# One instruction per 128 columns for scale, table and maximum of a windowed softmax, with slope tables that stay and a written order drawn up anew

## The chip, the core and the metric

The kernel runs on one core of a Trainium2 chip. The metric is the device time of one execution in microseconds, as the median of several runs. Five engines work side by side, each on its own queue in its own order: TensorE (PE; its weight loads are shown apart as PEld), VectorE (DVE), ScalarE (ACT), GpSimd (POOL) and SyncE (SP), which only issues transfers here.

## The reference, cut to what matters

```python
def _attn_ref(q, k, v):                      # 4 x 8 heads, 576 positions, 64 wide
    scores = scale * q @ k^T                 # scale = 1 / sqrt(64) = 0.125
    rel = pos[:, None] - pos[None, :]
    slopes = 2.0 ** (-8.0 * (arange(H) + 1) / H)      # 2 ** -(head + 1) for 8 heads
    scores = where((rel >= 0) & (rel < 128), scores - slopes * abs(rel), -1e9)
    attn = exp(scores - max(scores))
    return (attn / (sum(attn) + 1e-9)) @ v

x = heads side by side                       # 2304 x 512
x = (sigmoid(x @ w_gate) * (x @ w_val)) @ w_out       # 12 slices of 128 columns
out = ((x @ w1) * (x @ w2)) @ w3 @ w_out2
```

## The kernel before

The 2304 rows are 18 tiles of 128, in five blocks of 2, 4, 4, 4 and 4 tiles (`TILES`). Attention runs in 20 steps n = 0 to 19: five blocks times four pairs of heads (n = 4 * block + pair). `stage_s(n)` computes the scores of a step in sub-steps of two tiles and two heads, so n = 0 to 3 have one sub-step and the other 16 steps two each: 36 sub-steps. Of a sub-step the scores s lie in PSUM as two key blocks per tile. VectorE (1) copies with a mask, so that one block of 128 columns per tile and head holds the 128 keys of the window (L797, letter m), (2) multiplies 512 columns by the scale and adds a table (L801, letter t), (3) takes the maximum over 128 columns for four rows at once (L808, letter x), and for pairs 1 to 3 scales that maximum (L812). ScalarE takes four exponentials of 128 columns with their sums (L816, letter e). VectorE forms the reciprocal of the sums (L820, L821, letter s), GpSimd and ScalarE multiply by it (L826, L828, letter n). `stage_p` (L836) transposes the result on TensorE, ScalarE copies it out and GpSimd cuts it into its own and the previous key block; `stage_pv` multiplies by v into pv, and the result is split into a high part xth and a low part xtl, the sum of which is the input x of the first layer.

The table (`table`, `fill_table`) is made per block: for a block's 2 or 4 tiles and the two heads of pair 0. The other pairs use the same table: their scores are multiplied by 4 ** pair on the way in, and the exponential divides again. It takes 18 instructions of 128x256, 2 on ScalarE for block 0 and 16 on GpSimd.

Weights come as 64-bit words. `rounded` turns 128 rows of 512 of them into 32 bit numbers: one step on ScalarE (L195, letter a) and six on VectorE (L197 to L202, letter r), called a conversion below; then high and low parts are written (`wsl`, on ScalarE and GpSimd, letter c), or the result goes back to memory for later (`early`, from SP, letter u). The raw words are fetched by SP (L173, letter w). A name such as a_(6, 0) is slice 6 of the first layer, weight 0 (gate), and a_('ahead', 'o2', 3) a weight that is only needed later.

The first layer runs by groups of weight slices: slice 0, slice 1, then (2, 3), (4, 5) and so on, each over the five blocks. `gv` makes two products (L412), ScalarE a tanh of the first, and VectorE combines it with the second into g (L434, letter g), which sets its PSUM bank free. `down1` multiplies by the third weight into dn (L452) and VectorE adds it up in acc (L460, L462, letter d). Slices 0 and 1 run as fillers among the attention steps on TensorE.

What sets the order: TensorE follows the order of the program during attention. For the other engines `TURNS` holds one string of letters per engine; `line_up` chains the instructions marked by `turn` in the order of the letters, and a scheduler places everything else. Before, `line_up` is called when the fillers are done, ahead of the loop over the groups from (2, 3) on. From there the scheduler decides.

## Time and profile before

| | us |
|---|---|
| runs, median of 3 (lowest, highest) | 891.55 (889.65, 892.42) |
| the profiled execution | 895.77 |
| its span | 894.1 |

The profile is of the one execution of 895.77 us, 4.2 us above the median; 1.7 us of it lie outside the span. It tells for each engine when an instruction ran and what ended the idle time before it. "PEclk" is the clock that TensorE was granted, as a share of its higher level.

### The profile page before, as it was taken

How to read it: one execution, taken by the hardware profiler on the slowest of the kernel's cores; microseconds unless marked ns; L12 is line 12 of the kernel's file. 1: busy time of each engine (PE TensorE's matmuls, PEld its weight loads, DVE VectorE, ACT ScalarE, POOL GpSimd, SP SyncE). 2: the span in 40 equal slices, each digit the busy share in tenths (PEclk: the TensorE clock that was granted, in tenths of full speed). 3: DMA queues.
4: the chain of work that ended last, by engine and by line, in shares of the span. 5: the costliest groups of instructions: out<-in, count | busy, mean ns of one | idle time of the engine just before them, and what ended most of it. 6: DMA issues, size and time to landing. Idle time of an engine off the chain costs nothing.

```text
span 894.1 us, 12465 instructions
## 1 busy us (share of the span) xinstructions
PE 868.7 (97%) x4432; PEld 714.3 (80%) x4432; DVE 661.8 (74%) x1156; ACT 351.4 (39%) x853; POOL 311.7 (35%) x352
## 2 busy tenths in 40 slices
PE   6789999999999999999999999999999999999998
PEld 4567777788878888888888888878788888888886
DVE  5989997599997994994898954595548887643434
ACT  6888877432323322322422433342333424222120
POOL 4776664533315313322511211114535542021121
PEclk9999999999999999999999999999999999999999
DMA  5535441323451430350145421048434355654322
GB/s 172 177 124 183 157 161 56 128 79 123 154 179 56 167 128 1 122 178 20 67 162 181 152 87 48 25 148 299 167 140 166 118 199 201 223 189 154 136 77 95
DMA packets 40046, 120.61 MB, mean 135 GB/s; under 512 B 4400, under 2 KB 6448, under 8 KB 37936
## 3 DMA queue, kind: packets, MB, share of 16 engines
q1 hardware_dynamic: 38688, 105.01, 34.7%
q10 hardware_dynamic: 1296, 14.81, 3.9%
q8 instruction: 35, 0.57, 0.3%
q14 instruction: 27, 0.22, 0.1%
HBM read 87.82 MB, written 31.98 MB: 134 GB/s over the span
## 4 chain that ended last, share of the span: by engine, by line
PE 75%; DVE 16%; DMA 4%; issue 3%; ACT 1%; POOL 1%; SPq 0%; ACTq 0%; DVEq 0%; POOLq 0%
PE gv L412 22%; PE o L642 11%; PE dn L452 11%; PE pb L523 9%; PE pd L523 5%; PE pv L861 4%; PE w3o L373 3%; PE s L788 3%; PE lone L616 3%; PE pc L523 2%; PE pt L836 2%; DVE acc L462 2%; DVE g L434 1%; DMA _('ahead', 'w3', 4)_4938<-in_w_dram 1%; DVE xf L107 1%
## 5 line engine op out<-in xcount | busy, mean ns | idle before, releaser
L412 PE MATMUL gv<-xth,wsl 128*128 128x512 f32 (+1 forms) x960 | 281.9, 371 | 3.4 <-DVE g L434 2.8
L412 PEld LDWEIGHTS gv<-xth,wsl 128*128 128x128 f32 x960 | 175.9, 190 | 38.5 <-DVE g L434 3.8
L412 PE MATMUL gv<-xtl,wsl 128*128 128x512 f32 (+1 forms) x480 | 177.5, 370 | 1.5 <-DVE xtl L107 1.5
L110 POOL TENSOR_TENSOR gt<-g,gt 128x512 fp32r<-128x512 f32 (+1 forms) x60 | 77.4, 1290 | 240.2 <-ACT gt L104 240.2
L452 PE MATMUL dn<-gt,wsl 128*128 128x512 f32 (+1 forms) x720 | 154.5, 368 | 0.0
L452 PEld LDWEIGHTS dn<-gt,wsl 128*128 128x128 f32 x720 | 125.8, 189 | 23.4 <-DVE su L820 0.3
L412 PEld LDWEIGHTS gv<-xtl,wsl 128*128 128x128 f32 x480 | 91.3, 190 | 16.1 <-DVE xtl L107 1.7
L523 PE MATMUL pb<-xf,forms 128*128 128x512 f32 x384 | 97.8, 391 | 0.0
L462 DVE TENSOR_TENSOR acc<-acc,dn 128x512 f32<-128x512 f32 (+1 forms) x120 | 73.1, 625 | 16.3 <-PE dn L452 16.1
L523 PEld LDWEIGHTS pb<-xf,forms 128*128 128x128 f32 x384 | 70.8, 188 | 14.9 <-ACT xb L104 0.5
L434 DVE SCALAR_TENSOR_TENSOR g<-g,gv 128x512 f32<-128x512 f32 (+1 forms) x60 | 37.4, 627 | 44.1 <-PE gv L412 44.0
L104 ACT ACTIVATE gt<-g 128x512 fp32r<-128x512 f32 (+1 forms) x60 | 35.1, 587 | 80.0 <-DVE g L434 79.9
L816 ACT ACTIVATE sm<-sm,mn 128x128 f32<-128x128 f32 x144 | 56.1, 392 | 14.3 <-DVE mn L812 11.0
L652 DVE TENSOR_TENSOR acc<-acc,o 128x512 f32<-128x512 f32 x54 | 36.8, 683 | 32.8 <-PE o L642 32.7
L110 POOL TENSOR_TENSOR tp<-x,tp 128x512 fp32r<-128x512 f32 x16 | 21.2, 1325 | 86.8 <-ACT tp L104 86.7
L523 PE MATMUL pd<-xf,forms 128*128 128x512 f32 x192 | 48.9, 390 | 0.8 <-DVE xb L566 0.8
L642 PE MATMUL o<-outw,tp 128*128 128x512 f32 x192 | 48.0, 390 | 0.3 <-POOL tp L110 0.3
L642 PE MATMUL o<-outw,tq 128*128 128x512 f32 x192 | 48.2, 389 | 0.0
L427 ACT ACTIVATE g<-gv 128x512 f32<-128x512 f32 (+1 forms) x60 | 32.5, 547 | 34.3 <-PE gv L412 29.7
L373 PE MATMUL w3o<-wo,w3s 128*128 128x512 f32 x192 | 44.4, 390 | 0.4 <-ACT w3s L104 0.4
L523 PEld LDWEIGHTS pd<-xf,forms 128*128 128x128 f32 x192 | 36.0, 188 | 8.7 <-DVE xb L566 1.3
L826 POOL TENSOR_SCALAR sm<-sm,su 128x128 f32<-128x128 f32 x72 | 29.3, 416 | 38.5 <-DVE su L821 27.3
(797 smaller groups left out, 1467.1 us busy)
## 6 DMA issues: line engine op xcount, KB each, us to landing
formd<-forms ACTq DMA_DIRECT2D x8, 1792.0 KB, 7.4
outw<-outd SPq DMA_DIRECT2D x16, 512.0 KB, 5.6
forms<-formd SPq DMA_DIRECT2D x8, 1024.0 KB, 5.1
ldk<-in_k_dram SPq DMA_DIRECT2D x16, 320.0 KB, 3.5
ldv<-in_v_dram SPq DMA_DIRECT2D x16, 320.0 KB, 3.8
out_dram<-acc SPq DMA_DIRECT2D x18, 256.0 KB, 2.0
ldq<-in_q_dram SPq DMA_DIRECT2D x16, 256.0 KB, 4.4
outd<-w3o SPq DMA_DIRECT2D x8, 512.0 KB, 2.9
```

The costliest lines, as they stand in the source:

```text
L104: return nc.scalar.activation(dst, src, AF.Copy)
L110: nc.gpsimd.tensor_tensor(dst, src, hi.bitcast(F32), ALU.subtract)
L373: nc.tensor.matmul(acc2, w3s[u][:, wp, i * P : (i + 1) * P], wo2[kk][:, xp], start=(kk == 0 and wp == 0 and xp == 0), stop=(kk == NC2 - 1 ...
L412: nc.tensor.matmul(ps, wsl[i][:, s, wp, kk * P : (kk + 1) * P], xs[blk][xp][:, kk], start=(kk == 0 and wp == 0 and xp == 0), stop=(kk == N ...
L434: nc.vector.scalar_tensor_tensor(pr, pr, 1.0, pss[i, 1], ALU.add, ALU.mult)
L452: nc.tensor.matmul(ps, wsl[i][:, 2, wp, m * P : (m + 1) * P], t[:, xp], start=n == 0, stop=n == 3 * len(grp) - 1,)
L462: nc.vector.tensor_tensor(a, a, ps, ALU.add)
L523: nc.tensor.matmul(ps, forms[i][:, a, wp, kk * P : (kk + 1) * P], xf[n, j][:, xp, kk], start=first and kk == 0 and (wp, xp) == PASSES[0], ...
L642: nc.tensor.matmul(ps, ts2[n, i][blk][:, xp, tt * P : (tt + 1) * P], outw[i][:, wp], start=k == 0, stop=k == 3 * len(grp) - 1,)
L652: nc.vector.tensor_tensor(a, a, ps, ALU.add)
L816: nc.scalar.activation(y, y, AF.Exp, bias=mn[:, j : j + 1], scale=1.0 / up, accum_out=su[:, j : j + 1])
L861: nc.tensor.matmul(ps[c, a:b], loads[n]["v"][:, j + 1, c], s["cp", h][:, m0 : m0 + b - a], start=j == -back, stop=j == nt - 1, skip_group_ ...
```

## The change

`tensor_reduce`, the scaling of the maximum and `scalar_tensor_tensor` go. In their place stand four `tensor_tensor_reduce` per sub-step, one for each 128 columns: each adds a table to the scores, multiplies by -0.125 and takes the minimum, which is the negated maximum. The built program shows each as two VectorE instructions, one of 128x128 and one of 128x1 that writes the minimum. The factor 4 ** pair is gone; instead each head has a table `slope` of its own, with one 128-column part for each of the four kinds of tile, made once. It takes 16 instructions of 128x256: 2 on ScalarE, 14 on GpSimd, nearly all at the very start. `base` has 4 parts instead of 7, so three copies on ScalarE go. `TURNS` is drawn up anew, and `line_up` comes two groups later, after group (4, 5), so that the written order now also covers groups (2, 3) and (4, 5).

```diff
-        "mxtsxxogsmsdtxsxddssdsosgdddoorrdrrdrdrrgddrrgdddrrdrgdddd"
+        "rggdddd"
+LINED = 3
...
-        base = spool.tile([P, 7, P], F32, name="base", bufs=1)
-        PAIRS = {"nf": 0, "fn": 1, "nn": 2, "nc": 3, "ca": 4, "an": 5}
+        base = spool.tile([P, 4, P], F32, name="base", bufs=1)
+        slopes = [cpool.tile([P, 4, P], F32, name=f"slope{head}") for head in range(2 * NPAIR)]
...
+        def table(pair, kinds):
+            for head in (2 * pair, 2 * pair + 1):
+                c = 8.0 * 2.0 ** -(head + 1)
+                to, by = slopes[head][:, kinds], base[:, kinds]
+                with turn("T"):
+                    if pair == 0 and kinds.start == 0:
+                        nc.scalar.activation(to, by, AF.Copy, scale=c)
+                    else:
+                        nc.gpsimd.tensor_scalar(to, by, c, 1.0, ALU.mult, ALU.mult)
...
                 with turn("t"):
-                    nc.vector.scalar_tensor_tensor(
-                        x[:, g].rearrange("p g u k -> p g (u k)"), ps[:, :, 1].rearrange("p g u k -> p g (u k)"),
-                        0.125 * up, tabs[blk][:, g].rearrange("p g u k -> p g (u k)"), ALU.mult, ALU.add,
-                    )
+                    for j in range(4):
+                        head, u = 2 * pair + j // 2, j % 2
+                        kind = "fnca".index(KINDS[t0 + 2 * tp + u])
+                        nc.vector.tensor_tensor_reduce(
+                            x[:, 2 * tp + j // 2, u], ps[:, j // 2, 1, u], slopes[head][:, kind],
+                            -0.125, 3.0e38, ALU.add, ALU.min, mn[:, j : j + 1],
+                        )
-                with turn("x"):
-                    nc.vector.tensor_reduce(
-                        mn, x[:, g].rearrange("p g u k -> p (g u) k"), axis=AX.X, op=ALU.max, negate=True
-                    )
-                    if pair:
-                        nc.vector.tensor_scalar(mn, mn, 1.0 / up, None, ALU.mult)
...
-                            y, y, AF.Exp, bias=mn[:, j : j + 1], scale=1.0 / up, accum_out=su[:, j : j + 1]
+                            y, y, AF.Exp, bias=mn[:, j : j + 1], scale=-1.0, accum_out=su[:, j : j + 1]
...
-        table(0)
+        for pair in range(NPAIR):
+            table(pair, slice(0, 2))
...
                         consts2()
-                if n % NPAIR == NPAIR - 2 and n // NPAIR + 1 < NBLK:
-                    table(n // NPAIR + 1)
+                    for pair in range(NPAIR):
+                        table(pair, slice(2, 4))
...
     while queue:
         convert_next()
-    line_up()
...
             convert(1 if blk == 0 else 3)
+        if gi == LINED:
+            line_up()
```

What the written order does is seen at three places. The first is VectorE at step n = 8, from its first masked copy on. Before (s_0_707 and s_1_712 are its two sub-steps, sm the softmax tile, mn the maxima, su the sums):

```order
L797 COPY_PREDICATED s_0_707<-mask,s_0_707 128x2x256
L820 TENSOR_SCALAR su_1_623<-su_1_623 128x4
L821 RECIPROCAL su_1_623<-su_1_623 128x4
L801 SCALAR_TENSOR_TENSOR sm_706<-s_0_707,tab_475 128x512
L797 COPY_PREDICATED s_1_712<-mask,s_1_712 128x2x256
L808 TENSOR_REDUCE mn_0_719<-sm_706 128x4
L197 TENSOR_SCALAR a_(1, 0)_655<-a_(1, 0)_655 128x512
L801 SCALAR_TENSOR_TENSOR sm_706<-s_1_712,tab_475 128x512
```

After, where the tiles are s_0_730, s_1_735, sm_729 and mn_0_741, and the second copy of each pair of heads' rows that read alike is left out:

```order
L789 COPY_PREDICATED s_0_730<-mask,s_0_730 128x2x256
L113 TENSOR_TENSOR xtl_611<-pv_716,xth_610 128x512
L798 ISA sm_729,mn_0_741<-s_0_730,slope_94 128x128
L798 ISA mn_0_741 128x1
...
L798 ISA sm_729,mn_0_741<-s_0_730,slope_95 128x128
...
L789 COPY_PREDICATED s_1_735<-mask,s_1_735 128x2x256
```

Two 512-column instructions per sub-step became four pairs. Ahead of this place stand 7 conversions now (the seventh but for its last step), those of slices 0 and 1 and of a_('ahead', 2, 0), where 3 stood before; the conversion of a_(1, 0), which begins here before, is long done.

The second place is VectorE in group (2, 3) of the first layer at the g of block 4 (its two slices). Before:

```order
L201 SCALAR_TENSOR_TENSOR s_(6, 1)_3277<-raw_(6, 1)_3150,s_(6, 1)_3277 128x512
L202 TENSOR_TENSOR a_(6, 1)_3276<-a_(6, 1)_3276,s_(6, 1)_3277 128x512
L200 TENSOR_SCALAR s_(7, 1)_3290<-a_(7, 1)_3289 128x512
L201 SCALAR_TENSOR_TENSOR s_(7, 1)_3290<-raw_(7, 1)_3164,s_(7, 1)_3290 128x512
L202 TENSOR_TENSOR a_(7, 1)_3289<-a_(7, 1)_3289,s_(7, 1)_3290 128x512
L434 SCALAR_TENSOR_TENSOR g_4_2850<-g_4_2850,gv_4_1_2854 128x512
L434 SCALAR_TENSOR_TENSOR g_4_2852<-g_4_2852,gv_4_1_2871 128x512
```

After (g_4_2893 and g_4_2895):

```order
L468 TENSOR_TENSOR acc_2_1698<-acc_2_1698,dn_2_2_2818 128x512
L440 SCALAR_TENSOR_TENSOR g_3_2764<-g_3_2764,gv_3_1_2768 128x512
L440 SCALAR_TENSOR_TENSOR g_3_2766<-g_3_2766,gv_3_1_2785 128x512
L440 SCALAR_TENSOR_TENSOR g_4_2893<-g_4_2893,gv_4_1_2897 128x512
L208 TENSOR_TENSOR a_('ahead', 'o2', 3)_2857<-a_('ahead', 'o2', 3)_2857,s_('ahead', 'o2', 3)_2858 128x512
L203 TENSOR_SCALAR a_('ahead', 'o2', 4)_2963<-a_('ahead', 'o2', 4)_2963 128x512
```

The g of block 4 moved ahead of the conversions of slices 6 and 7 and of three of the 'ahead' weights; these now come in group (4, 5).

The third place is the head of SP's queue, which issues the first transfers. Before:

```order
L751 DMA ldk_95<-in_k_dram 128x128
L752 DMA ldk_95<-in_k_dram 128x256
L173 DMA raw_(0, 0)_111<-in_w_gate_dram 128x1024
L764 DMA boot<-in_k_dram 128x2x128
L751 DMA ldk_100<-in_k_dram 128x128
```

After:

```order
L746 DMA ldk_103<-in_k_dram 128x128
L747 DMA ldk_103<-in_k_dram 128x256
L746 DMA ldk_108<-in_k_dram 128x128
L747 DMA ldk_108<-in_k_dram 128x256
L750 DMA ldq_109<-in_q_dram 128x256
L179 DMA raw_(0, 0)_119<-in_w_gate_dram 128x1024
L759 DMA boot<-in_k_dram 128x2x128
L179 DMA raw_(0, 1)_121<-in_w_val_dram 128x1024
```

The keys and queries of n = 1 moved ahead of the first raw weights (before, three of them come behind these), and raw (0, 1) moved ahead of the rest of the boot transfers, which bring n = 2 and 3. On TensorE the order is the same through all of attention.

## Rows read from the trace of the kernel before

**Rows 1.** Page, part 1: busy time, share of the span, instructions of TensorE.
```profile
PE 868.7 (97%) x4432; PEld 714.3 (80%) x4432; DVE 661.8 (74%) x1156; ACT 351.4 (39%) x853; POOL 311.7 (35%) x352
```

**Rows 2.** Windows of 25 us: stretch, busy PE, PEld, DVE, ACT, POOL (x instructions), PEclk, DMA.
```profile
0.00:25.00 25.00, 15.98 (x76) 10.04 (x76) 14.81 (x35) 15.52 (x59) 11.41 (x35) 1.00 0.58 185
25.00:50.00 25.00, 19.85 (x138) 14.04 (x139) 22.68 (x53) 21.03 (x80) 20.22 (x37) 0.93 0.48 164
50.00:75.00 25.00, 22.57 (x164) 16.22 (x166) 22.35 (x52) 21.52 (x80) 16.27 (x29) 0.93 0.31 108
75.00:100.00 25.00, 24.41 (x190) 19.24 (x188) 24.16 (x59) 20.37 (x74) 18.22 (x29) 1.00 0.66 224
...
250.00:275.00 25.00, 22.44 (x114) 19.29 (x113) 22.81 (x41) 7.55 (x14) 5.95 (x5) 0.93 0.45 148
```

**Rows 3.** Timelines between 51 and 62 us, VectorE, then TensorE; in brackets the idle time before.
```profile
53.03 0.69 DVE L797 COPY_PREDICATED s<-mask,s 128x512 f32<-128x512 int32 x1 [1.05 <-PE s L788]
...
61.87 2.10 PE L836 MATMUL pt<-ident,sm 128*128 128x128 f32 x7 [0.98 <-POOL sm L826]
```

**Rows 4.** VectorE's lines, shapes apart: count, busy us, mean ns, idle before.
```profile
L797 DVE COPY_PREDICATED s<-mask,s 128x512 f32<-128x512 int32 x36 | 24.6, 685 | 16.8 <-PE s L788 16.8
L801 DVE SCALAR_TENSOR_TENSOR sm<-s,tab 128x512 f32<-128x512 f32 x36 | 24.5, 680 | 0.4
L808 DVE TENSOR_REDUCE mn<-sm 128x4 f32<-128x512 f32 x36 | 24.4, 678 | 0.3
...
L462 DVE TENSOR_TENSOR acc<-acc,dn 128x256 f32<-128x256 f32 x24 | 9.4, 410 | 0.3 <-PE dn L452 0.3
```

**Rows 5.** VectorE's timeline near 80 us: start, duration, instruction.
```profile
79.89 0.68 DVE L808 TENSOR_REDUCE mn<-sm 128x4 f32<-128x512 f32 x1
80.49 0.41 DVE L460 COPY acc<-dn 128x256 f32<-128x256 f32 x1
80.82 0.17 DVE L821 RECIPROCAL su<-su 128x4 f32<-128x4 f32 x1
80.90 0.14 DVE L812 TENSOR_SCALAR mn<-mn 128x4 f32<-128x4 f32 x1
80.95 0.42 DVE L198 TENSOR_SCALAR a_(1, 2)_947<-a_(1, 2)_947 128x512 uint32<-128x512 uint32 x1
```

**Rows 6.** Timeline of the first tile: VectorE, then ScalarE.
```profile
5.92 0.70 DVE L797 COPY_PREDICATED s<-mask,s 128x512 f32<-128x512 int32 x1 [4.99 <-PE s L788]
...
6.53 0.66 ACT L195 ACTIVATE a_(0, 0)_190<-raw_(0, 0)_111 128x512 f32<-128x512 f32 x1 [1.90 <-DMA raw_(0, 0)_111<-in_w_gate_dram]
6.73 0.69 DVE L801 SCALAR_TENSOR_TENSOR sm<-s,tab 128x512 f32<-128x512 f32 x1
...
8.18 0.40 ACT L816 ACTIVATE sm<-sm,mn 128x128 f32<-128x128 f32 x1 [1.00 <-DVE mn L808]
...
8.49 0.19 ACT L816 ACTIVATION_READ_ACCUMULATOR sm<-sm,mn 128x1 f32 x1
8.58 0.39 ACT L816 ACTIVATE sm<-sm,mn 128x128 f32<-128x128 f32 x1
```

**Rows 7.** Waits of TensorE after 110 us: in total us, times, longest.
```profile
PE gv L412 <- DVE g L434: 2.8, 3, 1.9
```

**Rows 8.** VectorE's timeline near 268 us.
```profile
268.06 0.69 DVE L202 TENSOR_TENSOR a_(7, 1)_3289<-a_(7, 1)_3289,s_(7, 1)_3290 128x512 f32<-128x512 f32 x1
268.67 1.28 DVE L434 SCALAR_TENSOR_TENSOR g<-g,gv 128x512 f32<-128x512 f32 x2
```

**Rows 9.** Windows of 3 us around that wait, columns as in group 2.
```profile
266.00:269.00 3.00, 1.46 (x13) 1.26 (x11) 2.86 (x6) 0.00 (x0) 0.00 (x0) 1.00 0.51 175
269.00:272.00 3.00, 2.60 (x15) 2.60 (x16) 3.00 (x6) 1.61 (x3) 1.91 (x2) 0.70 0.52 175
272.00:275.00 3.00, 3.00 (x16) 2.81 (x16) 1.09 (x3) 1.10 (x3) 1.35 (x2) 0.73 0.00 0
```

**Rows 10.** VectorE's timeline: g of block 0 in groups (2, 3) and (4, 5).
```profile
198.54 0.41 DVE L434 SCALAR_TENSOR_TENSOR g<-g,gv 128x256 f32<-128x256 f32 x1
...
272.25 0.42 DVE L434 SCALAR_TENSOR_TENSOR g<-g,gv 128x256 f32<-128x256 f32 x1
```

## The prediction

> **What bounds the kernel now.** I read the page first: TensorE is busy for 868.7 of 894.1 us [rows 1], so that all a change off TensorE can win is its 25 us of idle time and the stretches in which its clock is not the full one. The windows tell where these lie [rows 2]: in the first 100 us TensorE lacks 9.0, 5.2, 2.4 and 0.6 us per window, 17.2 in all, and from 250 to 275 us it lacks 2.6 again. In three of these windows the granted clock is 0.93. The rest of the span offers little, save the tail after 875 us, which the change doesn't touch. In the first stage VectorE is the partner to watch: busy for 14.8 of the first 25 us, then for 22 to 24 of each 25 [rows 2]. The chain of waits runs through it from 21.7 to 40.1 us and again from 53.03, the first masked copy of step n = 8, to the reciprocals of that step; then GpSimd normalizes and TensorE starts its transposes at 61.87 [rows 3]. So the question is whether VectorE gets through its list sooner. At 250 to 275 us it is another question: what stands in front of g.

> **The price of the new pair.** VectorE's instructions overlap, so two prices can be read. From start to start, a 512-column instruction takes 0.60 us, one of 256 columns 0.33, one of 4 columns 0.05 to 0.08 [rows 5]. That is 0.27 us per 256 columns and 0.06 on top, so 128 columns take 0.20 and the 128x1 write about 0.07. From end to end, the rows say 680 ns for 512 and 410 for 256 columns [rows 4], so 0.28 for 128, and 0.17 for a small one [rows 5]. A pair lies between 0.27 and 0.45 us. No VectorE instruction in this trace writes an accumulator, so the low end is an assumption; its nearest row is ScalarE's, where the accumulator read follows its exponential and delays the next one by only 0.09 us, 8.49 to 8.58, though it lasts 0.19 [rows 6]. A price under 0.27 I exclude, as the columns alone take 0.13 and both parts have to be issued. I take 0.27.

> By sub-step: before, 0.60 + 0.60 + three quarters of 0.08 (L812 runs for three pairs of heads in four) = 1.26 us; after, 4 x 0.27 = 1.08. That is 0.18 less, 6.5 us over 36. At 0.45 it is 1.80, 0.54 more, 19 us over 36.

> [...]

> **Attention, part by part.** Up to the first masked copy of n = 8 the written order now asks for more of VectorE, not less. Before, 12 sub-steps at 1.26, 12 masked copies at 0.60, three conversions of 2.8 (three steps at 0.33 and three at 0.60 each) and about 3.9 of others (22 small ones, four of 256 columns and one of 512 for xtl, one for g) make 34.6 us of work by 53.03: 18.4 us were unused. After, 12 at 1.08, the same copies, conversions 19.0 (six, and all but the last step of a seventh) and about 4.0 of others make 43.2: 8.6 more. It fits only into the unused time. Of that, 5.9 us go before the first scores are there [rows 6]. About 2 more go because the second pair stands behind the first step of the conversion of raw (0, 0), which now comes as SP's sixth transfer and not its third; its ScalarE step ran at 6.53 before [rows 6] and I put it at 8. And a dependent instruction right behind its source starts late: 0.81 us instead of 0.60 from the copy to the next [rows 6]; some 15 such places and a few waits for TensorE cost 2 to 3. That gives 43.2 + 10 to 11 = 53 to 54 us for n = 8, against 53.03: nothing won, up to 1 lost. From there VectorE is ahead, since four conversions that were still to come are done: up to the first copy of n = 12 its list is 1.7 us shorter than before, up to n = 15 about 12. There TensorE already lacked only 0.6 us per window [rows 2]. Within the steps the exponentials can start after the first pair and not after 512 columns and a maximum, about 1 us sooner on the path to the reciprocal, and boot, queries of n = 1 and pv start a little sooner. I take -1 us for attention, with ends at -6 (most of the 7.6 idle between 25 and 75 goes) and, with the pair at 0.45, about +12: 20 sub-steps up to n = 12 at 4 x 0.18 make 14.4, and the 1.7 come off.

> The tables cost nothing: 14 GpSimd instructions where 16 were, at their end before GpSimd's first normalization, in time in which it was idle (11.4 of 25 us busy [rows 2]); without that cover one would cost 0.3 to 0.4 us. ScalarE loses two copies of the base, 0.3 us each, at a time when it waits for transfers.

> **The stall at 250 to 275 us.** After 110 us TensorE waits for g three times, 2.8 us in all, 1.9 at the longest [rows 7]. The timeline shows the cause: PSUM is full until VectorE has formed the g of block 4, and g starts at 268.67 directly after the last of a row of conversion steps for slices 6 and 7 [rows 8], which the next group but one needs first. Behind the wait the granted clock is 0.70 and 0.73 for two windows of 3 us [rows 9], 0.9 and 0.8 us of work lost. The new order puts these g ahead of those conversions. I take 2.8 + 1.7 = 4.5 us as gone; what is late next is TensorE itself. The moved conversions land in group (4, 5), where VectorE's list from the first g of block 0 to the same g a group later is about 56 us long. TensorE takes some 74 for a group, the g of block 0 starting at 198.54 in the first and at 272.25 in the second [rows 10]. So they fit, but many six-step conversions now stand in one row, each step behind its source, and an order fixed by hand waits at each step for its transfer. I charge 1 us for new waits of this kind, with ends at 0 and 4.5.

> **Sum.** -1 - 4.5 + 1 = -4.5 us: 895.8 becomes 891.3 for an execution like the profiled one, and 891.55 becomes 887.0 for the median of the runs.

> **The rivals.** (a) Slower: the pairs pay from end to end, 0.45 us. The place is VectorE between 21 and 86 us. From 0.27 up, each 0.01 costs 20 x 4 x 0.01 = 0.8 us there, so the gain of 4.5 is used up at a pair of 0.33, and from 0.36 the kernel is slower by over 0.3%. At 0.45: 891.55 + 12 - 3.5 = 900. For it: two instructions became eight, and an accumulator's write may have to wait for the last column. Against it: the overlap shown for all other VectorE instructions, and ScalarE's 0.09. [...]
> (b) Same: attention comes out level or a little late and the stall at 256 to 269 us only changes its place, since SP, ScalarE and VectorE now wait in a fixed order. 891.55 - 0 to 1 = 891.
> (c) Faster still: the time between 25 and 75 us, which TensorE spends idle or at 0.93, mostly goes, 5 to 6 us, as the shorter way to the reciprocal counts and the conversions fill only gaps: 891.55 - 6 - 4.5 + 1 = 882.

> **How the numbers follow.** A measurement of this kernel tells about 0.3% from no change, so faster is under 888.9 and slower over 894.2. The forecast has 0.40, (c) 0.22, (b) 0.23, (a) 0.15. The forecast's own spread is about 3 us either way: 0.30 of it is faster, 0.08 same, 0.02 slower. (b) is same with 0.17 and slower with 0.04, faster with 0.02; (a) is slower with 0.13, same with 0.02. Together 0.54 faster, 0.27 same, 0.19 slower. For 8 in 10 the range goes from 879, past (c), to 898, which holds (b) and the milder half of (a).

> **What would show it.** Of the pair: VectorE's start to start between two ISA rows of L798 is 0.27 if I am right, 0.45 in (a). Of attention: TensorE's busy time in the windows up to 100 us adds to 82.8 now and to 83 to 85 then, and the first transposes of n = 8 come between 61 and 63 us. Of the stall: no wait of gv for g over 0.5 us between 250 and 275, and a granted clock of 1.00 there. Wrong would be a pair far over 0.3, a step of VectorE that waits for a transfer while g stands behind it, or GpSimd's tables still running when the first reciprocal is there.

## The result and the profile after

The changed kernel takes 896.28 us in the median (895.68 to 897.16, 4 runs), the one before 890.69 (889.65 to 892.42, 4 runs); the ratio is 1.0055 with an interval of 1.0038 to 1.0072. It is 5.6 us slower, where 4.5 us faster was forecast: inside the range of 879 to 898, on the other side of no change.

The two profiled executions hide this: their spans are 894.1 and 893.9 us. The one of before is slower than any of its 4 runs, the one of after is the fastest of its own 4. So times are compared by the runs here, and the profiles are read for places.

Windows after, columns as in [rows 2]:

```profile
0.00:25.00 25.00, 15.16 (x73) 9.06 (x73) 16.00 (x68) 14.52 (x51) 17.83 (x46) 1.00 0.63 205
25.00:50.00 25.00, 19.62 (x128) 13.58 (x128) 22.42 (x87) 21.44 (x82) 18.19 (x30) 0.86 0.51 174
50.00:75.00 25.00, 20.18 (x151) 13.85 (x149) 22.94 (x94) 21.86 (x81) 16.57 (x27) 1.00 0.53 174
75.00:100.00 25.00, 24.99 (x193) 19.82 (x192) 20.36 (x84) 20.10 (x76) 15.18 (x28) 1.00 0.52 171
...
250.00:275.00 25.00, 25.00 (x135) 21.66 (x134) 17.93 (x30) 6.31 (x11) 7.73 (x6) 1.00 0.34 112
...
375.00:400.00 25.00, 24.44 (x108) 19.74 (x107) 23.81 (x42) 6.72 (x11) 4.51 (x3) 1.00 0.43 147
400.00:425.00 25.00, 23.36 (x124) 19.60 (x124) 20.55 (x35) 6.54 (x12) 6.67 (x6) 1.00 0.35 117
```

TensorE lacks 20.05 us in the first 100 us, where it lacked 17.2 [rows 2]; 2.4 of these 2.9 us go between 50 and 75 us. The stall at 250 to 275 us is gone, clock and all, but 0.56 and 1.64 us are missing between 375 and 425 us, where nothing was missing before.

VectorE's timeline at the first masked copy of n = 8:

A pair takes 0.21 us from start to start: the write of the minimum lasts 0.08, but the next pair starts with it. The copy comes at 57.50, where it came at 53.03 [rows 3], though each of the 12 sub-steps ahead of it costs 0.84 us and no longer 1.26.

Where the first time is lost, in the timelines of ScalarE and TensorE:

```profile
24.79 0.69 ACT L201 ACTIVATE a_(1, 0)_678<-raw_(1, 0)_327 128x512 f32<-128x512 f32 x1 [1.29 <-DMA raw_(1, 0)_327<-in_w_gate_dram]
...
28.41 0.33 PE L825 MATMUL pt<-ident,sm 128*128 128x128 f32 x1 [1.58 <-POOL sm L815]
29.84 0.90 PE L825 MATMUL pt<-ident,sm 128*128 128x128 f32 x3 [1.11 <-POOL sm L815]
```

and in windows of 5 us, columns as in [rows 2]:

```profile
25.00:30.00 5.00, 1.52 (x7) 0.76 (x7) 4.67 (x18) 4.75 (x20) 3.15 (x6) 0.89 0.25 72
30.00:35.00 5.00, 5.00 (x25) 3.45 (x27) 3.34 (x10) 3.46 (x13) 3.46 (x7) 0.50 0.59 208
```

ScalarE waits for the raw words of slice 1 with exponentials queued behind, the normalization comes late, TensorE is idle for 3.5 of 5 us, and behind that its granted clock is 0.50 in every window of 0.5 us from 29.0 to 35.5, the lower of the two levels in this profile (0.50 and 1.00). The scores of n = 5 start at 32.16 instead of 27.77.

Between 50 and 75 us GpSimd stands in the way, in the timelines of GpSimd and TensorE:

```profile
50.99 1.27 POOL L116 TENSOR_TENSOR wsl<-a_(1, 1)_774,wsl 128x512 fp32r<-128x512 f32 x1 [1.08 <-ACT wsl L110]
52.24 0.72 POOL L815 TENSOR_SCALAR sm<-sm,su 128x128 f32<-128x128 f32 x2
...
52.67 1.11 PE L825 MATMUL pt<-ident,sm 128*128 128x128 f32 x6 [1.58 <-POOL sm L815]
```

The reciprocal for this normalization was done at 49.63. But GpSimd's order puts the low part of a_(1, 1) first, for which it waits 1.08 us and works 1.27, and TensorE waits 1.58. The part of a_(1, 2) at 57.79 does the same and is followed by a wait of 1.21 us.

### The profile page after: what moved, and what is told of

Its sections match the earlier page's. It is cut to its first block, busy times and chain, and to the rows that moved or that the text cites. A ratio compares the mean times of both kernels' runs of the same rounds, so it can differ in the third digit from the quotient of the medians.

```text
span 893.9 us, 12642 instructions
## 1 busy us (share of the span) xinstructions
PE 866.4 (97%) x4432; PEld 711.1 (80%) x4432; DVE 648.1 (73%) x1345; ACT 349.0 (39%) x850; POOL 309.2 (35%) x350
## 4 chain that ended last, share of the span: by engine, by line
PE 80%; DVE 10%; DMA 4%; issue 2%; ACT 2%; POOL 1%; SPq 1%; ACTq 0%; POOLq 0%; DVEq 0%
PE gv L418 27%; PE dn L458 12%; PE o L648 11%; PE pb L529 9%; PE pd L529 5%; PE w3o L379 3%; PE pv L850 3%; PE s L782 3%; PE lone L622 3%; PE pc L529 2%; PE pt L825 2%; DVE acc L468 1%; DMA boot<-in_q_dram 1%; DVE xf L113 1%; DVE acc L500 1%
## 5 line engine op out<-in xcount | busy, mean ns | idle before, releaser
L782 PE MATMUL s<-ldk,ldq 64*128 64x256 f32 x272 | 38.1, 421 | 7.2 <-DMA ldk<-in_k_dram 3.8
```

Source lines behind the costliest of these rows:

```text
L782: nc.tensor.matmul(ps[:, h, :, u], ld["q"][r, t * P : (t + 1) * P], ld["k"][r, t * P : (t + 2) * P], start=True, stop=True, skip_group_che ...
```

## The experiments

Ratios are to the kernel before on the same chip, with 95% intervals; "copy" is the first masked copy of n = 8.

**The kernel before, once more** (no edit). 

> The kernel before, unchanged, once more. Theory A (the stall at 250 to 275 us and the low granted clocks of its profile are in every execution): a second profile shows the wait of gv for g of about 1.9 us near 269 us and the granted clock of 0.93 in three windows again, span near 894. Theory B (they came with the one profiled execution of 895.77, which is 4 us above the runs of 889.65 to 892.42): the second profile lacks at least one of them and its span is 888 to 891. Under B the term of -4.5 us of the sum rested on something that most executions don't pay.

Measured: 891.26 us, 1.0002 (0.9989 to 1.0014). Theory A for the profiled execution: the second profile, of a span of 892.2, has three windows at 0.93 again and the same stall, in its window and in TensorE's timeline.

```profile
250.00:275.00 25.00, 22.32 (x113) 19.09 (x112) 21.30 (x38) 6.24 (x12) 6.59 (x6) 0.93 0.34 115
```

```profile
266.38 0.39 PE L412 MATMUL gv<-xth,wsl 128*128 128x256 f32 x1 [1.98 <-DVE g L434]
```

Its copy comes at 51.24 and its last pv starts at 162.6, 3.1 us earlier than in the first profile. So much two executions of one kernel differ in attention. For the other executions A is not shown: the profiled one took 893.93 us at a mean granted clock of 0.994, the other 11 took 889.50 to 892.76 at 0.996 to 1.000. Three windows of 25 us at 0.93 make 0.994 over the span, so none of the 11 had all three, and the 1.7 us that the sum counted for the clock behind the stall need not be in most executions.

**The order of the groups undone.**

```diff
-            line = [marked[engine, c].pop(0) for c in letters]
+            line = [marked[engine, c].pop(0) for c in letters if marked.get((engine, c))]
...
     while queue:
         convert_next()
+    line_up()
...
-        if gi == LINED:
-            line_up()
```

> The changed kernel, but the written order ends where it ended before, ahead of group (2, 3); the later letters are skipped and the scheduler decides there. Theory A (the 5.6 us were lost in attention, TensorE idle 20.1 us up to 100 us where it was 17.2): still 895 to 897. Theory B (they were lost in the newly written groups, where TensorE waits for g between 375 and 410 us for 2.2 us): 891 to 893.5. TensorE's idle time up to 100 us stays at 20 in both.

Measured: 895.22 us, 1.0036 (1.0023 to 1.0049); TensorE lacks 21.9 us up to 100 us. Theory A, with 1 to 2 us left for the groups (896.28 against 895.22, 1.0055 against 1.0036), though the intervals overlap. Attention is the main place.

**The instruction alone, in the old order.** On the run ahead, `TURNS` of before, with "tttt" for "t" and no "x" (the first letters of VectorE and SP):

```diff
-        "hmtrtrtrtrmrsrsrttttmrtttsrsrtmrtrtsmtttsort"
+        "hmttttmttttssmrttttrrssrmttttrsmsottttsrsmot"
...
-        "kkkkkwbwbbvkvkwvkvkw"
+        "kkwbkkkvvbbwkvkwkvkk"
```

> The one instruction per 128 columns and the lasting slope tables, but VectorE, ScalarE, GpSimd and SP in the order written before (each t of VectorE becomes four, each x goes; the tables stand at the head of GpSimd's queue) and the written order ending at the old place. By rows of the changed kernel a pair takes 0.21 us from start to start, so a sub-step takes 0.84 where it was 1.26. Theory A (VectorE's list sets the end of attention up to n = 12, and the new order spoilt the gain): 20 sub-steps x 0.42 = 8.4 us less work on that path, of which TensorE's 8.2 us idle between 25 and 100 us can be won; 884 to 888. Theory B (VectorE's list isn't the bound, the instruction gains nothing by itself): 889 to 892, as before.

Measured: 888.99 us, 0.9967 (0.9952 to 0.9982), copy at 48.80. By the ratio the instruction is worth 2.9 us by itself (1.8 by the medians). A held in its sign, but the time lies just short of B's 889: 8.4 us less of VectorE's work gave a third at most.

**The instruction taken apart in the new order.**

```diff
-                        nc.vector.tensor_tensor_reduce(
-                            x[:, 2 * tp + j // 2, u], ps[:, j // 2, 1, u], slopes[head][:, kind],
-                            -0.125, 3.0e38, ALU.add, ALU.min, mn[:, j : j + 1],
-                        )
+                        y = x[:, 2 * tp + j // 2, u]
+                        nc.vector.scalar_tensor_tensor(
+                            y, ps[:, j // 2, 1, u], -0.125, slopes[head][:, kind], ALU.mult, ALU.add
+                        )
+                        nc.vector.tensor_reduce(mn[:, j : j + 1], y, axis=AX.X, op=ALU.min)
```

> The changed kernel with its order kept, but each of the four instructions taken apart again into a multiply-add of 128 columns and a minimum over them (tables scaled for it). By start to start that is 0.20 + 0.20 = 0.40 us where the pair takes 0.21: 0.19 x 4 x 36 = 27 us more of VectorE's time, 15 us of it up to n = 12. Theory A (VectorE's list sets the end there): 8 to 15 us slower than the changed kernel, 904 to 911. Theory B (in the new order VectorE has slack, and other engines and transfers are waited for): 896 to 901.

Measured: 913.88 us, 1.0251 (1.0233 to 1.0269), beyond A. The timeline shows why:

```profile
24.73 0.28 DVE L800 SCALAR_TENSOR_TENSOR sm<-s,slope 128x128 f32<-128x128 f32 x1
25.05 0.29 DVE L803 TENSOR_REDUCE mn<-sm 128x1 f32<-128x128 f32 x1
25.26 0.28 DVE L800 SCALAR_TENSOR_TENSOR sm<-s,slope 128x128 f32<-128x128 f32 x1
```

0.32 + 0.21 = 0.53 us, since the minimum needs the result ahead of it; I had left that wait out of the 0.40. The change's instruction is right, then. The order must be wrong.

**The order divided in two: softmax letters and conversion letters.** First merged by counting letters, then by the times that the letters had on the chip. Edits of `TURNS` alone, on the order that ends at the old place (the first letters of VectorE; old order, then the first two runs):

```diff
-        "hmttttmttttssmrttttrrssrmttttrsmsottttsrsmot"
+        "hmtrtrtrtmrrrrttttssmrtttrrtssmrtrtttsmsotrt"
+        "hmttttmssrttttmrrtttrsstmrttsmtttsotttrssmtt"
...
+        "hmttttrrrmrtttrtssrmrttttrssrmrtttrtrsmrsotr"
```

> One instruction per 128 columns; the softmax letters of all engines in the order written before, as in the fused kernel in the old order (888.99), but the letters of the conversions (ScalarE's first step, VectorE's six, the parts, SP's fetches) at the places of the new order, counted by the softmax letters around them. The written order ends at the old place. Last pv was at 158.4 us there and at 169.9 us with the new order throughout (895.22). Theory A (the early conversions cost it: seven instead of three ahead of step n = 8, 11 us more of VectorE on the path of the first steps): 893 to 897, last pv at 165 or later. Theory B (the order of the softmax letters themselves costs it): 887 to 890.5, last pv before 161.

Measured: 933.51 us, 1.0463 (1.0430 to 1.0495): neither. By counting, steps came ahead of their data (TensorE waited 6.9 us for a maximum from 8.4 us on and 4.8 for values from 78.7 on), so it tells nothing of the two theories.

> One instruction per 128 columns, the softmax letters in the new order, the conversions' letters (on ScalarE, VectorE, GpSimd and SP) at the places of the old order; both orders were merged by the times that their letters had on the chip, brought to one scale by the starts of the scores of each step. The written order ends at the old place. Theory W (VectorE's first copy of n = 8 comes some 16 us after the listed work, in either order: 57.5 = 40.6 + 16 + 0.9 in the changed kernel, 48.8 = 29.8 + 18 + 0.9 in the fused kernel in the old order): the work is 29.8 again, the copy comes at 46 to 50, and the time is 0.995 to 0.999 of before. Theory S (the order of the softmax letters costs it): the copy at 55 or later, 1.003 to 1.006.

> The opposite of the run ahead, merged in the same way: softmax letters in the old order, conversions at the new places. Theory W: the listed work ahead of n = 8 is 40.6, the copy comes at 56 to 59, and the time is 1.003 to 1.008 of before. Theory S: the copy at 47 to 51 and 0.995 to 0.999.

| copy, ratio | conversions at old places | at new places |
|---|---|---|
| softmax in old order | 48.8, 0.9967 | 61.5, 1.0111 (1.0084 to 1.0139) |
| softmax in new order | 52.6, 0.9981 (0.9969 to 0.9994) | 57.3, 1.0036 |

Each copy is read from one execution, and two of the kernel before are 1.8 us apart (53.03 and 51.24). The conversions' new places cost 0.55% in the new softmax order and 1.4% in the old one. The new softmax order costs 0.14% at the old places, with overlapping intervals, and gains 0.75% at the new ones. So the places are the cause, as W says. Its constant of 16 us fell, and with it its copies and the time of the second run, which lies past its 1.008: what stands beside the listed work is 17 to 23 us (below).

**One letter.** The changed kernel, ScalarE:

```diff
-        "poeeaennpoepeene"
+        "poeeennpoeapeene"
```

> The changed kernel with one letter of ScalarE moved: the first step of the conversion of a_(1, 0), which waited 1.29 us for its transfer (landed at 24.70) with exponentials and normalizations queued behind it, goes six instructions later. Theory A (that wait is what starts TensorE's waits for GpSimd of 1.58 and 1.11 us at 28.4 and 29.8 and the granted clock of 0.50 behind them): 1.3 us of wait and about 2 us of slow clock go, 892 to 894.5. Theory B (VectorE's list sets the pace anyway, the wait is one of several): 895 to 896.5, scores of n = 5 still later than 31 us (26.4 in the old order).

Measured: 895.57 us, 1.0042 (1.0025 to 1.0059), scores of n = 5 at 30.74, copy at 56.14. Theory B by its time (the scores came just ahead of its 31 us): the wait is one of several.

**VectorE's share of an early conversion**, added alone to the old order (letter q, 23 times), then taken alone out of the new one:

```diff
+        with turn("q"):
+            for i in range(23):
+                if i % 6 in (0, 1, 3):
+                    nc.vector.tensor_scalar(more[0], more[0], 0.5, 1.0, ALU.mult, ALU.add)
+                else:
+                    nc.vector.scalar_tensor_tensor(more[0], more[0], 0.5, more[1], ALU.mult, ALU.add)
...
+        if key in ((1, 0), (1, 1), (1, 2), ("ahead", 2, 0)):
+            x, y, a, s, low, high = (ap[:, 0:8] for ap in (x, y, a, s, low, high))
```

> The fused kernel in the old order (0.9967 of before; first copy of n = 8 at 48.8), with 23 instructions of 128x512 on scratch tiles added on VectorE alone, a chain of 3 one-input and 3 two-input steps like a conversion's, at the places where the new order has the 23 conversion steps that it brings ahead of n = 8. No transfer, no ScalarE step and no part on GpSimd comes with them, and no later work goes. Theory V (what costs is VectorE's time ahead of n = 8): 23 steps make 10.8 us, the copy of n = 8 comes at 57 to 61 and the time is 1.003 to 1.010 of before. Theory R (what costs is the rest of an early conversion: transfers, ScalarE's step and GpSimd's part in the way): the copy before 54, the time below 1.000.

> The new order with the written order ending at the old place (1.0036 of before; first copy of n = 8 at 57.3), with VectorE's six steps of the conversions of a_(1, 0), a_(1, 1), a_(1, 2) and a_('ahead', 2, 0) cut from 512 to 8 columns; the other columns of these four weights are left unconverted. Transfers, ScalarE's steps, GpSimd's parts and the whole order stay. Theory V: 23 steps at 0.06 instead of 10.6 us, some 9 us less ahead of n = 8, the copy at 47 to 50 and the time 0.993 to 0.998 of before. Theory R: the copy after 54, the time above 1.000.

Measured: added 1.0098 (1.0063 to 1.0134), copy at 61.66, theory V, a little past its numbers for the copy; cut 1.0033 (1.0013 to 1.0054), copy at 55.87, theory R. VectorE's time ahead of n = 8 is enough to lose it, but not the only thing that does.

**Each part of the early conversions cut**, in the new order: VectorE's steps of all seven (the list of keys longer), the parts (`still`, a constant tile for TensorE), the transfers (EARLY stands for the seven keys; the steps read a constant tile):

```diff
-                nc.sync.dma_start(t.rearrange("p c t -> p (c t)"), src.bitcast(U32))
+                some = slice(0, 8 if key in EARLY else 2 * DM)
+                nc.sync.dma_start(t.rearrange("p c t -> p (c t)")[:, some], src.bitcast(U32)[:, some])
...
+        if i < GF:
+            wsl[i] = still
+            small = xpool.tile([P, 2, 8], F32R, name=f"small{i}_{c}")
+            return small[:, 0], small[:, 1]
```

> The new order with the written order ending at the old place (1.0036 of before; scores of n = 5 at 32.2, first copy of n = 8 at 57.3), VectorE's six steps cut from 512 to 8 columns in all seven conversions that stand ahead of n = 8, those of slice 0 too; their other columns are left unconverted. 41 steps at 0.06 instead of 19 us, some 16 us less for VectorE. Theory V (the loss up to n = 5 is VectorE's steps of slice 0, which the run with four conversions cut left in place): scores of n = 5 at 26 to 29, the copy of n = 8 at 46 to 51, below 0.999 of before. Theory R (transfers, ScalarE's steps or GpSimd's parts set it without VectorE): n = 5 after 30, the copy after 54, above 1.000.

> The same new order with VectorE's steps whole, but the high and low parts of slices 0 and 1 (ScalarE 0.53 us and GpSimd 1.27 us for each weight from start to start) cut from 512 to 8 columns; TensorE multiplies by a constant tile there, so the first two slices' results are wrong. Five weights lie ahead of n = 8: 2.4 us less on ScalarE, 6 us less on GpSimd, which normalizes the softmax behind them. Theory C (these parts delay the normalization): the copy of n = 8 at 54 or earlier, 1.001 of before or less. Theory not C: the copy at 56 or later, 1.002 or more.

> The same new order with the transfers of the raw words of the seven weights ahead of n = 8 cut to 8 words a row, and their conversions reading a constant tile, so that no step waits for a transfer and the boot and the queries have the queues for themselves; these weights are wrong. All steps of ScalarE, VectorE and GpSimd stay. Theory D (the transfers set it: the boot's queries at 12.1, ScalarE's wait of 1.3 us for raw (1, 0)): scores of n = 2 at 10 or earlier, n = 5 at 29 or earlier, below 1.000 of before. Theory not D: n = 5 after 30, the copy of n = 8 at 55 or later, 1.001 or more.

> The new order once more (1.0036 of before), with both cuts that helped: VectorE's steps of the seven early conversions cut to 8 columns (alone 1.0001, copy of n = 8 at 52.4) and their transfers cut to 8 words a row (alone 0.9993, copy at 54.2). What is left of an early conversion is its step on ScalarE and its parts on ScalarE and GpSimd. Theory A (the two hold TensorE at different places): the gains add, 0.9955 to 0.9975, the copy of n = 8 at 47 to 50. Theory B (both are in one chain of waits, so that the second cut finds little left): 0.9980 to 1.0000, the copy at 51 or later.

| new order with | ratio | scores of n = 5 | copy |
|---|---|---|---|
| nothing cut | 1.0036 | 32.2 | 57.3 |
| VectorE's steps cut | 1.0001 (0.9982 to 1.0019) | 28.5 | 52.4 |
| parts cut | 1.0101 (1.0083 to 1.0120) | 31.2 | 55.4 |
| transfers cut | 0.9993 (0.9974 to 1.0012) | 28.8 | 54.2 |
| VectorE's steps and transfers | 0.9949 (0.9930 to 0.9967) | 24.9 | 48.6 |

The transfers' cut met all three numbers of theory D (scores of n = 2 at 9.1), VectorE's met that of n = 5 and fell short of the other two. Each gives back about 0.4%, and the two add up to 0.87%, a little past the range of theory A of the last run. So they act as two losses at different places, not as one chain. The run with the parts cut isn't settled: its last pv starts at 167.9, 1.9 us earlier than with nothing cut (169.9), but behind it the span is 4.3 us longer (898.1 - 167.9 = 730.2 against 725.8). Its matmuls of L537 last 394 ns there, where the same ones lasted 391. They also last 394 ns in the profile of the run with the transfers cut, an execution of 894.51 us, 2.8 above that run's median; so the longer matmuls don't come with the parts' cut alone, and what makes them longer stays open. What the parts cost is not measured.

TensorE's busy time in the first 160 us (columns as in [rows 2]), in this order: before, changed, instruction alone, VectorE's steps and transfers cut.

```profile
0.00:160.00 160.00, 142.79 (x965) 105.94 (x966) 135.76 (x312) 124.47 (x453) 100.19 (x191) 0.98 0.43 144
```

```profile
0.00:160.00 160.00, 139.95 (x957) 103.05 (x958) 119.68 (x498) 122.12 (x447) 96.83 (x185) 0.98 0.44 144
```

```profile
0.00:160.00 160.00, 144.57 (x1022) 107.96 (x1024) 125.18 (x506) 124.21 (x455) 99.45 (x195) 0.99 0.46 152
```

```profile
0.00:160.00 160.00, 145.67 (x1022) 109.80 (x1024) 109.50 (x506) 125.61 (x456) 97.39 (x195) 0.98 0.40 129
```

In the changed kernel VectorE is busy 16 us less than before in this stretch, and TensorE has 2.8 us less done.

**The new groups behind the old attention** (the instruction alone, then the rest of the new letters and `LINED = 3`). 

> The fused kernel in the old order through attention (888.99), and behind that the newly written order of groups (2, 3) and (4, 5). Theory A (my term: the stall at 250 to 275 us, 1.6 us of waits in that kernel, goes and little comes): 885 to 887.5. Theory B (the stall only changes its place: TensorE waits for g between 375 and 410 us instead, 2.2 us in the changed kernel): 888 to 891, no wait for g over 0.5 us before 300 us and at least 1.5 us of them between 370 and 420.

Measured: 888.86 us, 0.9961 (0.9940 to 0.9982), level with 0.9967. Theory B, as its windows and waits after 160 us show:

```profile
250.00:275.00 25.00, 25.00 (x135) 21.67 (x134) 22.85 (x41) 5.06 (x10) 4.01 (x4) 1.00 0.45 147
375.00:400.00 25.00, 23.16 (x100) 18.10 (x98) 23.34 (x41) 6.82 (x11) 4.26 (x3) 1.00 0.55 181
400.00:425.00 25.00, 24.36 (x130) 20.83 (x129) 17.93 (x29) 8.35 (x17) 9.53 (x9) 1.00 0.15 44
```

```profile
PE gv L418 <- DVE g L440: 3.0, 5, 0.9
```

**A new head for SP**, with the instruction, and on the kernel before:

```diff
-        "kkwbkkkvvbbw"
+        "kkkkkbbbwvvw"
...
-        "khThThaeeeeeeepnn"
+        "khThTheeeeeeeapnn"
```

> The fused kernel in the old order (888.99), with SP's head drawn up so that keys and queries of n = 1 and all boot transfers come ahead of the raw weights, and ScalarE's first conversion step behind the exponentials of n = 0 and 1. There TensorE waits 2.6 us for the queries of n = 1 and 0.5 for the boot. Theory A (the early steps hang on these transfers): scores of n = 1 at 6.3 instead of 8.4, up to 2 to 3 us gained, 886 to 887.5. Theory B (by n = 5 VectorE's list decides again and the raw weights come later): 888 to 890.

> The kernel before with the new head of SP alone (keys and queries of n = 1 and all boot transfers ahead of the raw weights, ScalarE's first conversion step behind the first exponentials); no fused instruction. Theory A (the head's gain of 0.36% with the fused instruction is one of its own): 0.995 to 0.998 of before, scores of n = 1 at 6.3 instead of 8.0. Theory B (without the shorter softmax VectorE's list is late anyway): 0.999 to 1.001.

Measured: 886.28 us, 0.9931 (0.9913 to 0.9950), scores of n = 1 right behind those of n = 0, of n = 2 at 8.02, and copy at 46.09, theory A; on the kernel before 889.99 us, 0.9984 (0.9967 to 1.0001), copy at 49.98, between A and B. The head seems to pay more where the softmax is short (0.36% against 0.16%), but the interval of the second reaches no change, so this is not shown.

**That head and the new order of group (2, 3) alone** (`LINED = 2`). 

> The fused kernel in the old order with the new head of SP (0.9931 of before), and behind attention the new written order of group (2, 3) alone, so that the g of block 4 there come ahead of the conversions; from group (4, 5) on the scheduler decides. Theory A (the wait for g moves to wherever the delayed conversions meet the next g): no wait for g over 0.5 us up to 300 us, but 1.5 us or more of them later, and 0.991 to 0.995. Theory B (the stall belongs to the scheduler's order of group (2, 3) and is gone for good): less than 1 us of such waits in all, and 0.988 to 0.991.

Measured: 885.02 us, 0.9926 (0.9908 to 0.9944), the best here and 0.7% ahead of the kernel before; but not apart from 0.9931. TensorE waits 0.7 us for g after 160 us, 0.5 at the longest, where it waited 2.1: theory B for the waits, while the time is A's. So the gain from that stall stays below what these runs can tell.

## Why the prediction was wrong

**The price: the row I took was too high, and what I excluded is what happens.** A pair takes 0.21 us, not 0.27; "under 0.27 I exclude" rested on adding the small write, and the write hides behind the next pair. By this term alone the kernel should have been faster than forecast. Rival (a) had the right sign with the wrong mechanism. That 896.28 lies inside the range is luck: its upper end stood there for a slow pair, and the pair was fast.

The fused form is the faster one here: one pair of 0.21 against two instructions of 0.53, and 17.6 us between the kernels (913.88 - 896.28). The number of instructions can't tell the two forms apart, as each is built as two per 128 columns.

**The step that failed: "It fits only into the unused time."** I listed 43.2 us of work ahead of n = 8 and let the unused 18.4 shrink to 10 or 11, for 53 to 54. With the true price the list is 40.3 (43.2 - 48 x 0.06), and the copy should have come at 50 to 51. The rest hardly shrank. Here the work is listed by the prediction's prices, with 0.21 for a pair (the expectations above count 0.2 to 0.3 more):

| | listed work | copy | rest |
|---|---|---|---|
| before | 34.6 | 53.0 | 18.4 |
| before, second execution | 34.6 | 51.2 | 16.6 |
| instruction alone | 29.6 | 48.8 | 19.2 |
| changed | 40.3 | 57.5 | 17.2 |
| new softmax, old conversions | 29.7 | 52.6 | 22.9 |
| old softmax, new conversions | 40.2 | 61.5 | 21.3 |

VectorE's busy time (third of the five) up to the copy, before and after, columns as in [rows 2], and its waits after, columns as in [rows 7]:

```profile
0.00:53.03 53.03, 38.86 (x243) 26.57 (x244) 39.36 (x93) 39.53 (x152) 34.06 (x75) 0.97 0.51 170
```

```profile
0.00:57.50 57.50, 40.56 (x248) 27.05 (x248) 45.59 (x181) 43.40 (x159) 40.03 (x83) 0.94 0.54 180
```

```profile
DVE s L789 <- PE s L782: 6.8, 5, 5.1
DVE a_(0, 0)_211 L203 <- ACT a_(0, 0)_211 L201: 2.0, 1, 2.0
DVE su L809 <- ACT sm L805: 1.6, 4, 0.7
```

Of the three terms of the 10 or 11, two came out as forecast: 6.0 us ahead of the first copy (5.9) and 2.0 for the first step of the conversion (2). The third, "2 to 3" for late starts and a few waits, measured 17.2 - 6.0 - 2.0 = 9.2. Of these, 1.7 are waits for later scores and 1.6 for sums from ScalarE; for 5.3 VectorE counts as busy (45.6 against 40.3), in steps that last longer than listed or whose successor doesn't start before their end. A conversion step at 15.22 us takes 0.99, where 0.33 is listed. Before, such steps already made 4.8 us (39.4 against 34.6): this part of the "unused" 18.4 was not free at all. My end of +12 for attention priced the pair alone; the work brought ahead got 0 to 1 us, and it is that term which was mis-sized: it made 4.5 us at the copy (57.50 against 53.03), with a cheaper pair. Attention ended later: the last pv starts at 167.5, where it started at 165.7 and 162.6 in two executions before, and at 158.4 with the instruction alone.

I also counted a conversion as VectorE's work only. The cuts show that its transfers cost as much as its steps (0.43% and 0.35%), in the timeline the 1.29 us of ScalarE and the boot, for which TensorE waits 3.7 us up to 12.08. And its parts stand on GpSimd ahead of normalizations that TensorE waits for (1.58 us up to 52.67, 1.21 up to 59.47). That the raw weights now go ahead of the boot I had taken for a small plus ("boot, queries of n = 1 and pv start a little sooner"). The queries do: TensorE starts n = 1 at 6.28 instead of 8.00. The boot doesn't: n = 2 starts at 12.08 instead of 11.35.

**The clock, which I counted only at the stall.** The mean granted clock of the changed kernel's 4 runs is 0.990 to 0.995. On one chip it is 0.990 to 0.996 in the 8 runs with the order of the groups undone, and 0.996 to 1.000 in 25 of the kernel before. As (1 - clock) x span, an estimate that takes TensorE as busy throughout, that makes 5.6 us against 2.4 in the mean. How much of the loss the clock is stays open: with one letter moved, the median clock is that of the kernel before on the same chip (0.996), and the time is still 1.0042.

**The catching up that I counted on came, and was worth little.** From 70 us on TensorE is busy without a wait over 0.1 us until 389; its 24.99 between 75 and 100 us, where it was 24.41, can't bring back what was lost before.

**The stall: right at its place, and it moved.** 2.56 us and a clock of 0.93 are gone at 250 to 275 us; 2.2 us of waits stand at 375 to 425, behind the conversions that were put off. My +1 for new waits was the small half of it; the end of 4.5 should have weighed more. And I took the 4.5 us, read from one execution of 895.77, off the median of 891.55 as well. The same exchange left the run with the old attention level. So this term failed as well: attention, forecast at -1, came out 3 to 4.5 us late (1.0036, and 895.22 against 890.76), and the groups, forecast at -4.5 + 1, between level and 2 us late. Each is about half of the 10 us between -4.5 and +5.6. Rival (b) named both, attention level or a little late and a stall that only changes its place; its price, 0 to 1 us of gain, was too kind.

**The tables cost next to nothing**: GpSimd's row of 13 ends at 9.4 us and its first normalization starts at 13.7. But the last one stands at 18.78, behind the first reciprocal (13.38), which I had named as a sign of being wrong, and ahead of a normalization for which TensorE waits 0.61 us up to 20.16. It can cost up to 0.5 us there (18.78 to 19.27); no run tries it.

**Of the tests named ahead**: TensorE's busy time up to 100 us was to be 83 to 85 and is 79.95; the transposes of n = 8 were to start between 61 and 63 and do so at 65.38; no wait over 0.5 us at 250 to 275 held.

## What to carry to other kernels

Unused time of an engine ahead of a date is not room: before work is brought forward, look at what ends each idle stretch, and count every part of that work, its transfers and its steps on the other engines, against the date. Test a faster instruction in the old order before a new order is drawn around it; here the two had opposite signs, -0.33% and +0.69% (1.0036 against 0.9967). And a stall that is cured by putting work off is to be looked for again where that work ends up.

## What the runs showed of the hardware

VectorE's accumulator write costs nothing in 123 of the 144 pairs of the changed kernel, with 0.00 us from its start to the next start, where, in the run with the instruction taken apart, a multiply-add and the minimum that needs its result take 0.51 to 0.53 us between 20 and 31 us, 0.30 to 0.32 more per 128 columns.

A one-input step of 512 columns lasts 0.41 to 0.43 us on VectorE in all 133 cases in the first 500 us of the changed kernel in which GpSimd did nothing beside it; beside GpSimd's two-input 128x512 it lasts 0.87 in the mean of 45, from 0.41 to 1.52. The same step twice, and GpSimd's row beside the second:

```profile
395.39 0.41 DVE L204 TENSOR_SCALAR a_('ahead', 12, 0)_4423<-a_('ahead', 12, 0)_4423 128x512 uint32<-128x512 uint32 x1
...
405.31 1.40 DVE L204 TENSOR_SCALAR a_(10, 1)_4559<-a_(10, 1)_4559 128x512 uint32<-128x512 uint32 x1
...
405.08 1.35 POOL L116 TENSOR_TENSOR gt<-g,gt 128x512 fp32r<-128x512 f32 x1 [13.56 <-ACT gt L110]
```

VectorE's step ends 0.28 us after GpSimd's (406.71 against 406.43). What makes it longer, no run shows.
